# The first batch's local attention in blocks of 32 queries and 38 keys, its pooled part added in PSUM, and its q and k loaded as 1.5 KB rows

## The chip, the core and the metric

The kernel runs on one core of a Trainium2 chip. The metric is the device time of one execution in microseconds (us), as the median of the runs. The engines are named as in the profile: PE (TensorE: matmuls and transposes), PEld (its weight loads), DVE (VectorE), ACT (ScalarE), POOL (GpSimd), SP (SyncE, which here only issues DMAs). PSUM has eight banks; a matmul writes there, and DVE or ACT read it out.

## The reference

Eight batches of attention with 8 heads, 576 positions and 64 numbers a head, all float32; then a layer norm and a feed-forward network over the joined heads.

```python
B, H, S, D = q.shape                      # 8, 8, 576, 64; factor = 4
q_d = q.reshape(B, H, S // 4, 4, D).mean(axis=3)      # k_d and v_d likewise
out_up = np.repeat(sm_attn(q_d, k_d, v_d), 4, axis=2) # full attention on the pooled ones
mask = np.abs(pos[:, None] - pos[None, :]) < 4        # local attention: 7 neighbours
scores = np.where(mask, scale * (q @ k.T), -1e9)
out_local = softmax(scores) @ v
x = (out_up + out_local).transpose(0, 2, 1, 3).reshape(B, S, 512)
xn = (x - mu) / np.sqrt(var + 1e-6) * g_ln
out = x + np.maximum(xn @ w_ch1, 0.0) @ w_ch2         # 512 -> 2048 -> 512
```

The two weight matrices come as float64 and are turned into float32 pairs (a high and a low part) in the kernel.

## The kernel before

**The whole.** The 8 x 576 = 4608 rows of x are 36 tiles of 128 rows. The feed-forward network goes over them in chunks: chunk 0 has 4 tiles (rows 0 to 511, nearly all of batch 0), chunk 1 has 2, the others 3 each. In a chunk, `up` (products named h, L1279) and `down` (acc, L1303) go over 16 blocks of the 2048 hidden columns. In chunk 0 each block's weights are still to be loaded (tiles s) and converted (hi, lo on ACT, DVE and POOL). Attention of the later batches is done between the network's products.

**The order.** A class `Plan` collects tasks: an engine, an estimated duration, the tasks it needs, a due time, and rooms (buffers) taken and given back: "u" (2 KB buffers), "a" (the 8 PSUM banks), "e" (wide buffers), "xx". It lays them out by due times and costs and writes each engine's program in that fixed order; each engine then works through its list and waits on semaphores. Where its layout leaves a gap on PE, it puts warm-up matmuls of the identity there (L205). The DMAs on SP are issued in the order of the list too, and each also waits for the DMA eight before it.

**Batch 0.** It stands ahead of all else, since chunk 0 needs it. Its q and k are loaded by tokens (`own_tokens`, L472: 128 tokens by 8 heads, pieces of 64 numbers), turned on PE by transposes (L479), summed in fours on DVE for the pooled attention and copied to `reg` by ACT. Local attention (`window`) goes by windows of two blocks, 64 queries by 64 keys each: a mask product (L541), scores (L550), exponentials, transposes (L582), times v (`times_v`, L601, with a column of ones whose result is the sum), and a division on DVE or ACT. The pooled attention (scores gs L955, transposes gt L1006, times v gv L1021) gives od. Since the 64 keys of a block give 58 queries, the windows don't lie on tiles of x: `expand` picks the rows with a 0/1 matrix named choice (ex L1119) and adds the pooled rows, repeated by a 0/1 matrix named spread (L1128), in one PSUM bank. Rows 512 to 575, half of tile 4, go by DMA: pooled rows to DRAM (ud, L1049), and x<-xl (L1227).

**Batches 1 to 7** (`pair`: qr and kr loads L709, DVE transposes, ls L754, lt L803, lv L821, a store xs<-xl to DRAM) are not edited. DVE's L831 writes xl, which lies in a room "e".

Their and the network's lines move only by the file's length: L205 becomes L209, L709 L714, L1279 L1245, L1303 L1269.

Of the kernel before, what the change touches and what calls it, by code (L numbers as in the profile page):

```python
# [9 lines left out]
F32 = mybir.dt.float32  # L10
# [129 lines left out]
def attention_then_ffn(  # L140
# [42 lines left out]
    TOKENS = ((0, 128), (128, 128), (256, 96), (340, 128), (468, 108))  # L183
    CUT = TOKENS[3][0]
    GROUPS = (0, 32, 64, 85, 117, SD)
    NU -= sum(SEP.values())
    SHIFTED = (0, 1, 2, 3)
# [31 lines left out]
    mask_b = const.tile([P, 2, 64], mybir.dt.bfloat16, name="mask_b")  # L219
# [25 lines left out]
    def copy_masks():  # L245
        nc.vector.tensor_copy(mask_b, mask.unsqueeze(1).broadcast_to([P, 2, 64]))
        nc.vector.memset(mask_b[64:, 1, 63:], NEG)

    SEL, SEL0 = 128, 376
    box_sel = []  # L250

    def make_choice():
        t = unit([P, 512], "choice")
        box_sel.append(t)
        nc.gpsimd.memset(t, 0.0)
        for c0, c1, firsts in ((0, SEL0, (EDGE, EDGE)), (SEL0, SEL0 + P, (0, EDGE))):
            for par in range(2):
                m = t[64 * par : 64 * par + 64, c0:c1]
                at = (SEL if c0 == 0 else 0) + HOP * par
                nc.gpsimd.affine_select(  # L260
                    out=m, in_=m, compare_op=ALU.not_equal, fill=1.0, base=at, pattern=[[-1, c1 - c0]],
                    channel_multiplier=1,
                )
                for base, sgn in ((-firsts[par], 1), (HOP + EDGE - 1, -1)):
                    nc.gpsimd.affine_select(
                        out=m, in_=m, compare_op=ALU.is_ge, fill=0.0, base=base, pattern=[[0, c1 - c0]],
                        channel_multiplier=sgn,
                    )

    SPREAD_LAST = FACTOR * 2 * GB  # L270

    def make_spread():
        t = wide([P, SPREAD_LAST + 2 * P], "spread")
        box_sel.append(t)
        nc.gpsimd.memset(t, 0.0)
        half = SPREAD_LAST // 2
        for par, c0, n, first in (
            (0, 0, half, 0), (1, half, half, 0), (0, SPREAD_LAST, P, 64 - GB), (1, SPREAD_LAST + P, P, 64 - GB)
        ):
            m = t[64 * par : 64 * par + 64, c0 : c0 + n]  # L280
            nc.gpsimd.memset(m, 1.0)
            for sgn in (1, -1):
                nc.gpsimd.affine_select(
                    out=m, in_=m, compare_op=ALU.is_ge, fill=0.0, base=FACTOR * first if sgn > 0 else EDGE - FACTOR * first,
                    pattern=[[sgn, n]], channel_multiplier=-sgn * FACTOR,
                )
# [20 lines left out]
    def window_at(i):  # L307
        return norm_at(0) - B0W - B0W_GAP * (2 - i)

# [15 lines left out]
    B0W, B0W_GAP, B0G, B0G_GAP = 5, 3, 8, 1.5  # L325
# [5 lines left out]
    EARLY_DUE = 40  # L331
# [122 lines left out]
    xt, piece = {}, {}  # L454
    chosen, own_moves = {}, []
    reg, turned_own, sums_own, vp, vp_done = {}, {}, [], {}, []
    gs = {}

    def own_tokens(u, nm):
        src = q if nm == "q" else k  # L460
        t0, n = TOKENS[u]
        part = int(t0 >= CUT)
        off = t0 - (CUT if part else 0)
        g0, g1 = GROUPS[u], GROUPS[u + 1]
        due = window_at(max(u - 1, 0))
        add = plan.add
        x = SimpleNamespace()
        by_act = nm == "k" and u < BY_ACT

        def load():  # L470
            x.raw = unit([P, H, D], f"{nm}n{u}")
            (nc.scalar if by_act else nc.sync).dma_start(  # L472
                x.raw[:n], src[0, :, t0 : t0 + n, :].rearrange("h c d -> c h d")
            )

        def turn():
            x.p = psa(f"l{nm}{u}").rearrange("p (c t) -> p c t", c=NPAIR)
            for pr in range(NPAIR):
                nc.tensor.transpose(  # L479
                    x.p[:, pr, :n], x.raw[:n, 2 * pr : 2 * pr + 2].rearrange("p h d -> p (h d)"), ident[:n, :n]  # L480
                )

        def sums():
            if u == 0:
                gs[nm] = wide([P, NPAIR, SD], f"gs{nm}")
            nc.vector.tensor_reduce(
                out=gs[nm][:, :, g0:g1],
                in_=x.p[:, :, : FACTOR * (g1 - g0)].rearrange("p c (g r) -> p c g r", r=FACTOR),
                axis=AX.X, op=ALU.add,
            )  # L490

        def turn_out(copy):
            if off == 0:
                width = S + 1 - CUT if part else TOKENS[2][0] + TOKENS[2][1]
                reg[nm, part] = work.tile([P, NPAIR, width], F32, tag="xx", bufs=NX, name=f"r{nm}{part}")
                if part:
                    nc.gpsimd.memset(reg[nm, part][:, :, width - 1 :], 0.0)
            copy(reg[nm, part][:, :, off : off + n], x.p[:, :, :n])
# [9 lines left out]
    def own_v(pr):  # L508
# [3 lines left out]
        def ones_v():  # L512
            vp[pr] = wide([P, NBLK, D + 1], f"vp{pr}")
            nc.gpsimd.memset(vp[pr][:, :, D], 1.0)
# [888 lines left out]
```

## Time and profile before

| | |
|---|---|
| median of 3 runs | 972.67 us (970.27 to 974.83) |
| profiled execution | 971.22 us, its span 969.5 us |
| PE busy in the span | 949.3 us (98%) |
| DVE, ACT, POOL busy | 568.2 (59%), 285.5 (29%), 210.6 us (22%) |
| mean granted clock of PE | 0.995 |

The span runs from the first to the last instruction of the profiled execution; 1.7 us of its time lie around it. A busy share is a sum over stages: warm-up matmuls count as busy, and the first 150 us differ from the rest.

### The profile page before, as it was taken

Reading aid. Unit: us, or ns where it says so; the run is one execution under the profiler, and the core shown is the slowest. Engines: PE = TensorE matmul, PEld = TensorE weight load, DVE = VectorE, ACT = ScalarE, POOL = GpSimd, SP = SyncE. Lnnn points to the kernel's source line nnn. Section 1 sums busy time; section 2 is a strip of 40 time slices with the busy share of each in tenths; the row PEclk is TensorE's granted clock in tenths of the full one; section 3 lists DMA queues with packets and bytes.
Section 4 is the critical chain, followed back from the end, with each engine's and each line's share of the span. In section 5 each row is a group of like instructions: output and inputs, shape, how many; then the busy total and the mean of one; then the engine's idle time right before and its main releaser. Section 6 shows DMA issues by size and latency. Waiting matters only on the chain.

```text
span 969.5 us, 22589 instructions
## 1 busy us (share of the span) xinstructions
PE 949.3 (98%) x8742; PEld 852.9 (88%) x8742; DVE 568.2 (59%) x1363; ACT 285.5 (29%) x757; POOL 210.6 (22%) x395
## 2 busy tenths in 40 slices
PE   9898989999999999999999999999999999999998
PEld 8787878999889989889988989899989989999997
DVE  5499755767565757567477567768467443233212
ACT  4787854223123132113123112213113121212110
POOL 7325323333212212222111011232022001110000
PEclk9999989999999999999999999999999999999999
DMA  8998986687787849788677797997786565432400
GB/s 172 176 276 203 274 221 166 192 226 197 211 190 192 235 140 232 235 225 215 216 188 181 200 244 203 248 267 202 217 200 190 161 196 159 162 107 68 163 1 33
DMA packets 311299, 183.88 MB, mean 190 GB/s; under 512 B 197080, under 2 KB 264600, under 8 KB 311192
## 3 DMA queue, kind: packets, MB, share of 16 engines
q1 hardware_dynamic: 304648, 169.33, 65.8%
q0 software_dynamic: 3680, 12.39, 4.2%
q8 instruction: 69, 1.13, 0.5%
q10 hardware_dynamic: 2864, 0.72, 0.4%
q14 instruction: 38, 0.31, 0.1%
HBM read 139.91 MB, written 42.34 MB: 188 GB/s over the span
## 4 chain that ended last, share of the span: by engine, by line
PE 85%; DMA 1%; DVE 1%; SPq 0%; issue 0%; ACT 0%; DVEq 0%; ACTq 0%
PE h L1279 39%; PE acc L1303 39%; PE lv L821 2%; PE gv L1021 2%; PE ls L754 1%; PE gs L955 1%; PE gt L1006 1%; DMA xs<-xl 1%; DMA qr<-in_q_dram 0%; PE px L1183 0%; PE lt L803 0%; DVE x L1308 0%; PE h L205 0%; SPq L709 0%; DVE gmx L963 0%
## 5 line engine op out<-in xcount | busy, mean ns | idle before, releaser
L1303 PE MATMUL acc<-hi,hx 128*128 128x512 f32 x768 | 260.0, 392 | 0.0
L1290 DVE SCALAR_TENSOR_TENSOR hx<-h,hx 128x384 fp32r<-128x384 f32 (+1 forms) x176 | 95.6, 543 | 269.9 <-ACT hx L1287 269.5
L1287 ACT ACTIVATE hx<-h 128x384 fp32r<-128x384 f32 (+1 forms) x176 | 84.8, 482 | 556.1 <-PE h L1279 364.7
L1303 PEld LDWEIGHTS acc<-hi,hx 128*128 128x128 f32 x768 | 144.1, 188 | 28.8 <-issue 1.0
L1303 PE MATMUL acc<-lo,hx 128*128 128x512 f32 x384 | 151.2, 394 | 0.0
L1279 PE MATMUL h<-xh,lo 128*128 128x384 f32 (+1 forms) x656 | 135.8, 329 | 0.5 <-ACT xh L1188 0.5
L1279 PE MATMUL h<-xh,hi 128*128 128x384 f32 (+1 forms) x656 | 132.1, 323 | 0.0
L1279 PE MATMUL h<-xlo,hi 128*128 128x384 f32 (+1 forms) x656 | 131.6, 322 | 0.0
L1279 PEld LDWEIGHTS h<-xh,lo 128*128 128x128 f32 x656 | 111.4, 190 | 11.4 <-ACT xh L1188 0.7
L1279 PEld LDWEIGHTS h<-xh,hi 128*128 128x128 f32 x656 | 111.5, 189 | 0.0
L1279 PEld LDWEIGHTS h<-xlo,hi 128*128 128x128 f32 x656 | 109.7, 190 | 0.1
L1303 PE MATMUL acc<-w,hx 128*128 128x512 f32 x384 | 96.5, 395 | 0.0
L1303 PEld LDWEIGHTS acc<-w,hx 128*128 128x128 f32 x384 | 70.6, 188 | 13.7 <-issue 0.8
L1303 PEld LDWEIGHTS acc<-lo,hx 128*128 128x128 f32 x384 | 72.2, 188 | 9.7
L1138 POOL TENSOR_TENSOR x<-x,up 128x512 f32<-128x512 f32 x32 | 41.1, 1290 | 181.0 <-DMA x<-xs 119.0
L1279 PE MATMUL h<-xh,w 128*128 128x384 f32 (+1 forms) x352 | 67.7, 334 | 0.0
L1279 PEld LDWEIGHTS h<-xh,w 128*128 128x128 f32 x352 | 61.7, 188 | 3.3
L421 POOL TENSOR_TENSOR lo<-s,hi 128x512 fp32r<-128x512 f32 x27 | 36.4, 1355 | 65.9 <-ACT hi L416 47.1
L1188 ACT ACTIVATE xh<-xy,gain 128x128 fp32r<-128x128 f32 x108 | 34.8, 394 | 18.3 <-DVE xy L1175 17.5
L978 ACT ACTIVATE ag<-gs,gmx 128x192 f32<-128x192 f32 x96 | 32.0, 430 | 25.0 <-DVE lrp L829 9.6
L1152 POOL TENSOR_TENSOR mv<-mv,neg_half 128x1 f32<-128x1 f32 x36 | 21.8, 605 | 77.3 <-DVE mv L1149 61.1
L408 DVE SCALAR_TENSOR_TENSOR s<-s 128x256 int32<-128x256 int32 x64 | 35.3, 560 | 4.0 <-ACT s L400 2.0
(175 smaller groups left out, 1226.3 us busy)
## 6 DMA issues: line engine op xcount, KB each, us to landing
w<-w SPq DMA_DIRECT2D x148, 256.0 KB
s<-in_moe_w_ch_dram SPq DMA_DIRECT2D x64, 256.0 KB
out_dram<-x SPq DMA_DIRECT2D x36, 256.0 KB
vwp<-in_v_dram SPq DMA_DIRECT2D x54, 160.0 KB
qr<-in_q_dram SPq DMA_DIRECT2D x112, 72.0 KB
kr<-in_k_dram SPq DMA_DIRECT2D x112, 72.0 KB
up<-ud SPq DMA_DIRECT2D x28, 256.0 KB
x<-xs SPq DMA_DIRECT2D x28, 256.0 KB
```

The costliest lines, as they stand in the source:

```text
L408: nc.vector.scalar_tensor_tensor(out=x.raw[0][:, 256 * i : 256 * (i + 1)], in0=pairs[:, :, 1], scalar=3, in1=pairs[:, :, 0], op0=ALU.logic ...
L421: eng.tensor_sub(lo, x.raw[0].bitcast(F32), x.hi.bitcast(F32))
L821: nc.tensor.matmul(x.pv[h2][hs, w], lhsT=x.at[js, w, hs], rhs=x.v[js, 2 * w + par], start=True, stop=True)
L978: nc.scalar.activation(to, of, AF.Exp, scale=POOLED_SCALE, bias=y.mx[:, h2, c : c + 1])
L1021: nc.tensor.matmul(y.pv[h2][64 * n : 64 * n + 64, c], lhsT=y.at[kb][ks, c0 : c0 + 64], rhs=x.v[ks, kb, pr], start=kb == 0, stop=kb == 2,)
L1138: nc.gpsimd.tensor_add(xt[n], xt[n], x.up)
L1152: nc.gpsimd.tensor_tensor(x.mv[:, 1:2], x.mv[:, 1:2], neg_half, op=ALU.pow)
L1188: nc.scalar.activation(into(xh, kc), pxt[n][:, kc], AF.Copy, scale=gain[:, kc : kc + 1])
L1279: nc.tensor.matmul(out, lhsT=wt[:, kc], rhs=rhs, start=n == 0, stop=n == 3 * KC - 1)
L1287: nc.scalar.activation(hx[c, f][0], ph[c, f][:, :tokens], AF.Relu)
L1290: nc.vector.scalar_tensor_tensor(out=hx[c, f][1], in0=ph[c, f][:, :tokens], scalar=0.0, in1=hx[c, f][0].bitcast(F32), op0=ALU.max, op1=ALU ...
L1303: nc.tensor.matmul(acc[c][j], lhsT=lt[:, ts], rhs=rt, start=f == 0 and n == 0, stop=last and n == 2)
```

## The change

**Loads and turning.** `own_qk` loads q and k by head: 96 partitions hold 6 positions each, so a row is 6 x 64 numbers, 1.5 KB. There are 16 such DMAs (ten issued by SP, six by ACT). To get the 64 numbers on partitions, PE multiplies each of the six 64-column slices by the identity (L463), for two heads and in two pieces (partitions 0 to 63 and 64 to 95): 192 products, written to every sixth column of PSUM. DVE sums and ACT copies from there.

**Local attention.** `near_scores` takes 32 queries by 38 keys, four blocks to a window, so that a window is a tile of x: four windows of four blocks and one of two. It divides on DVE in SBUF before the transposes. `assembled` multiplies by v (L615) and adds the pooled rows by spread into the same PSUM bank (L622, L629); `keep` copies it to x. The choice matrix, `expand`, the DMAs to ud of batch 0 and x<-xl of tile 4 are gone. v comes in 16 pieces of 48 rows in two parts (18 DMAs, two of them on POOL). Two of the six poolings of v may go to DVE. Six planner constants change.

```diff
+    BQ, BK = 32, 32 + 2 * EDGE
+    PER = 6
+    RAW = S // PER
+    HIGH = 64
+    LEFT, CUT = 356, 348
+    SPLIT = (LEFT - BQ - EDGE) // BQ + 1
+    VROWS = 48
+    V_FIRST = 8
...
+    B0G, B0G_GAP = 20, 4
+    OWN_AT, OWN_V, OWN_V2, OWN_NEAR, OWN_GAP, OWN_END = -40.0, -2.0, 16.0, 10.0, 3.0, 4.0
...
-    EARLY_DUE = 40
+    EARLY_DUE = 25
...
-    LEAD1 = 40
+    LEAD1 = 35
...
-    G1 = 22
+    G1 = 20
...
-    W_GAP = 12
+    W_GAP = 13
...
+        def load(h2, by):
+            x.raw[h2] = unit([P, PER * D], f"{nm}n{pr}_{h2}")
+            by.dma_start(x.raw[h2][:RAW], src[0, 2 * pr + h2].rearrange("(g r) d -> g (r d)", r=PER))
+
+        def turn(n):
+            p0, p1 = ((0, HIGH), (HIGH, RAW))[n]
+            x.p[n] = psa(f"l{nm}{pr}_{n}")[:, : PER * (p1 - p0)]
+            for r in range(PER):
+                for h2 in range(2):
+                    nc.tensor.matmul(
+                        x.p[n][64 * h2 : 64 * h2 + 64].rearrange("p (g r) -> p g r", r=PER)[:, :, r],
+                        lhsT=x.raw[h2][p0:p1, r * D : (r + 1) * D], rhs=ident[p0:p1, p0:p1], start=True, stop=True,
+                    )
...
+            if n:
+                copy(reg[nm, 1][:, pr, PER * HIGH - CUT : S - CUT], x.p[n])
+            else:
+                copy(reg[nm, 0][:, pr, EDGE:], x.p[n][:, :LEFT])
+                copy(reg[nm, 1][:, pr, : PER * HIGH - CUT], x.p[n][:, CUT:])
...
+                q.dma_start(
+                    to[:VROWS, 1:], bass.AP(head.tensor, head.offset + (BQ - EDGE) * D, [[D, VROWS], [BQ * D, nb - 1], [1, D]])
+                )
+                return
+            q.dma_start(
+                to[:VROWS], bass.AP(head.tensor, head.offset + (BQ * m0 - EDGE) * D, [[D, VROWS], [BQ * D, nb], [1, D]])
+            )
...
-        def load():
-            x.raw = unit([P, H, D], f"{nm}n{u}")
-            (nc.scalar if by_act else nc.sync).dma_start(
-                x.raw[:n], src[0, :, t0 : t0 + n, :].rearrange("h c d -> c h d")
-            )
...
-        def turn():
-            x.p = psa(f"l{nm}{u}").rearrange("p (c t) -> p c t", c=NPAIR)
-            for pr in range(NPAIR):
-                nc.tensor.transpose(
-                    x.p[:, pr, :n], x.raw[:n, 2 * pr : 2 * pr + 2].rearrange("p h d -> p (h d)"), ident[:n, :n]
-                )
...
+                    x.ps[h2], lhsT=ident_b[:, :rows], rhs=near_b[:, variant].unsqueeze(1).broadcast_to([P, NPAIR, BK]),
                     start=True, stop=False,
                 )
...
-                    for par, c0 in enumerate(cols):
+                    for n, m in enumerate(blocks):
+                        part = int(m >= SPLIT)
+                        c0 = BQ * m - (CUT if part else -EDGE)
                         nc.tensor.matmul(
-                            x.ps[h2][64 * par : 64 * par + 64, pr], lhsT=qt[ds, pr, c0 : c0 + 64],
-                            rhs=kt[ds, pr, c0 : c0 + 64], start=False, stop=pr == NPAIR - 1,
+                            x.ps[h2][BQ * n : BQ * (n + 1), pr], lhsT=reg["q", part][ds, pr, c0 : c0 + BQ],
+                            rhs=reg["k", part][ds, pr, c0 - EDGE : c0 - EDGE + BK], start=False, stop=pr == NPAIR - 1,
                         )
...
+            nc.vector.reduce_sum(r, a, axis=AX.X)
+            nc.vector.tensor_scalar_add(r, r, 1e-9)
+            nc.vector.reciprocal(r, r)
+            nc.vector.tensor_mul(a, a, r.unsqueeze(2).broadcast_to([rows, H, BK]))
...
+                for h2 in range(2):
+                    js = slice(64 * h2, 64 * h2 + BK)
+                    for n, m in enumerate(blocks):
+                        part = int(m >= V_FIRST)
                         nc.tensor.matmul(
-                            x.pv[n][hs, pr], lhsT=x.at[js, pr, hs], rhs=vp[pr][js, blocks[m]], start=True, stop=True
+                            x.px[h2][BQ * n : BQ * (n + 1), pr], lhsT=x.at[js, pr, BQ * n : BQ * (n + 1)],
+                            rhs=vp[pr, part][js, m - V_FIRST * part], start=pr == 0, stop=False,
...
+            for h2 in range(2):
+                for hg in range(2):
+                    if i < 3:
+                        nc.tensor.matmul(
+                            x.px[h2][:, 2 * hg : 2 * hg + 2], lhsT=spread[0][:, i * P : i * P + rows],
+                            rhs=od[hg][:, :2, h2], start=False, stop=hg == 1,
+                        )
+                        continue
+                    for par in range(2):
+                        c0 = (S - 3 * P) * par + P * (i - 3)
+                        nc.tensor.matmul(
+                            x.px[h2][:, 2 * hg + par], lhsT=spread[1][:, c0 : c0 + rows], rhs=od[hg][:, 2, h2],
+                            start=False, stop=hg == 1 and par == 1,
+                        )
+
+        def keep():
+            xt[i] = unit([P, DM], f"x{i}")
+            for h2 in range(2):
+                nc.scalar.copy(xt[i][:rows].rearrange("p (c h d) -> p h c d", h=2, d=D)[:, h2], x.px[h2])
...
-                    nc.tensor.matmul(
-                        x.up[:, es], lhsT=box_sel[0][:, c0 : c0 + P], rhs=y.xl.rearrange("p h d -> p (h d)")[:, es],
-                        start=e == 0, stop=False,
-                    )
-                for pr in range(2 if n == NOWN - 1 else 1):
-                    c0, rhs, to = n * P, od[hg][:, :2], x.up[:, es]
-                    if n == NOWN - 1:
-                        c0, rhs = SPREAD_LAST + P * pr, od[hg][:, 2]
-                        to = x.up[:, hg * 256 + pr * P : hg * 256 + (pr + 1) * P]
-                    nc.tensor.matmul(to, lhsT=box_sel[1][:, c0 : c0 + P], rhs=rhs, start=False, stop=pr == 1 or n < NOWN - 1)
...
-                    def move(y=y, n1=n1, p0=p0, r0=r0, m=m):
-                        if n1 not in xt:
-                            xt[n1] = unit([P, DM], f"x{n1}")
-                        nc.sync.dma_start(xt[n1][p0 : p0 + m], y.xl[r0 : r0 + m].rearrange("p h d -> p (h d)"))
...
+        if n < NOWN:
+            t = kept_own[n]
```

**The start of PE's program.** k and q of the first group or pair are lk and lq; kn and qn are the loaded rows. Before:

```order
L205 MATMUL lk_140<-ident 128x128 x8
L479 MATMUL lk_140<-ident,kn_93 128x128 x4
L479 MATMUL lq_157<-ident,qn_95 128x128 x4
L205 MATMUL lk_170<-ident 128x128 x4
L479 MATMUL lk_170<-ident,kn_97 128x128 x4
L205 MATMUL lq_185<-ident 128x128 x4
L479 MATMUL lq_185<-ident,qn_99 128x128 x4
```

and after (twelve such products make a piece):

```order
L209 MATMUL lk_0_134<-ident 128x128 x8
L463 MATMUL lk_0_134<-ident,kn_0_83 64x64
L463 MATMUL lk_0_134<-ident,kn_1_81 64x64
L463 MATMUL lk_0_134<-ident,kn_0_83 64x64
L463 MATMUL lk_0_134<-ident,kn_1_81 64x64
```

The warm-up matmuls between the first turns are gone, and a piece of four transposes is now twelve products of 64 x 64 or 64 x 32.

**Where tile 0 of x is made, on PE.** at holds the turned attention, vp is v, od the pooled result; before, xl is the divided local result. Before:

```order
L582 MATMUL lt_812<-ident,la_618 128x128 x4
L582 MATMUL lt_817<-ident,la_712 128x128 x4
L1119 MATMUL ex_829<-xl_650,choice 128x256
L1119 MATMUL ex_829<-xl_710,choice 128x256
L1128 MATMUL ex_829<-od_769,spread 128x256
L1119 MATMUL ex_829<-xl_650,choice 128x256
```

and after:

```order
L615 MATMUL ex_0_916<-vp_0_85,at_871 32x64 x4
L615 MATMUL ex_1_917<-vp_0_85,at_871 32x64 x4
L615 MATMUL ex_0_916<-vp_0_523,at_871 32x64 x4
L615 MATMUL ex_1_917<-vp_0_523,at_871 32x64 x4
L615 MATMUL ex_0_916<-vp_0_565,at_871 32x64 x4
L615 MATMUL ex_1_917<-vp_0_565,at_871 32x64 x4
L615 MATMUL ex_0_916<-vp_0_575,at_871 32x64 x4
L615 MATMUL ex_1_917<-vp_0_575,at_871 32x64 x4
L622 MATMUL ex_0_916<-od_738,spread_169 128x128
L622 MATMUL ex_0_916<-od_858,spread_169 128x128
L622 MATMUL ex_1_917<-od_738,spread_169 128x128
L622 MATMUL ex_1_917<-od_858,spread_169 128x128
```

What was times v, a division elsewhere, and a selection is now 32 products of 32 x 64, with the four pooled products straight behind them.

**SP's queue behind the loads of v.** s_0 and s_1 are the first weight blocks, qr and kr are of batch 1. Before:

```order
L519 DMA vp_105<-in_v_dram 64x10x64 x2
L519 DMA vp_107<-in_v_dram 64x10x64 x2
L519 DMA vp_112<-in_v_dram 64x10x64 x2
L519 DMA vp_114<-in_v_dram 64x10x64 x2
L709 DMA qr_454<-in_q_dram 32x18x32 x4
L709 DMA kr_509<-in_k_dram 32x18x32 x4
L386 DMA s_0_0_556<-in_moe_w_ch_dram 128x2x256
L386 DMA s_0_1_557<-in_moe_w_ch_dram 128x2x256
```

and after:

```order
L534 DMA vp_1_585<-in_v_dram 48x10x64
L534 DMA vp_1_590<-in_v_dram 48x10x64
L534 DMA vp_1_631<-in_v_dram 48x10x64
L534 DMA vp_1_674<-in_v_dram 48x10x64
L376 DMA s_0_0_836<-in_moe_w_ch_dram 128x2x256
L376 DMA s_0_1_837<-in_moe_w_ch_dram 128x2x256
L376 DMA s_1_0_845<-in_moe_w_ch_dram 128x2x256
L376 DMA s_1_1_846<-in_moe_w_ch_dram 128x2x256
L714 DMA qr_866<-in_q_dram 32x18x32 x4
L714 DMA kr_961<-in_k_dram 32x18x32 x4
L381 DMA s_0_0_1057<-in_moe_w_ch_dram 128x512
L381 DMA s_0_1_1058<-in_moe_w_ch_dram 128x512
```

The first two blocks' weights now stand ahead of the loads of batch 1, and more DMAs stand ahead of both.

## Rows read from the trace of the kernel before

**Rows 1.** Busy times by stretch of the span: PE, PEld, DVE, ACT, POOL.
```profile
0.00:60.00 60.00, 54.03 (x874) 48.54 (x875) 36.88 (x109) 38.29 (x117) 28.99 (x91) 0.97 0.95 192
60.00:136.00 76.00, 69.86 (x759) 61.31 (x758) 63.40 (x143) 59.06 (x156) 32.49 (x34) 1.00 0.91 242
```

**Rows 2.** PE's waits, by what it waited for.
```profile
PE gt L1006 <- DVE lrp L829: 4.6, 2, 4.3
PE lv L601 <- DMA vp<-in_v_dram: 2.8, 3, 1.6
```

**Rows 3.** The warm-up matmuls (L205) by stretch; PE, PEld.
```profile
60.00:100.00 40.00, 3.37 (x24) 2.91 (x24) 1.00 0.93 237
...
sum 970.00, PE 23.32 PEld 21.29; mean PE 3.33 PEld 3.04
```

**Rows 4.** PE from the start to the network's first product: start, duration, instruction.
```profile
1.52 3.79 PE L205 MATMUL lk<-ident 128*128 128x128 f32 x16 [1.52 <-POOL ident masks.py:199]
5.09 1.06 PE L479 MATMUL lk<-ident,kn 128*128 128x128 f32 x4
...
7.14 1.06 PE L205 MATMUL lk<-ident 128*128 128x128 f32 x8
8.03 0.60 PE L479 MATMUL lk<-ident,kn 128*128 128x128 f32 x4
...
16.33 0.38 PE L541 MATMUL ls<-mask_b,ident_b 128*128 128x256 bf16 x2
16.65 0.70 PE L550 MATMUL ls<-rk,rq 64*64 64x64 f32 x32
17.27 0.59 PE L479 MATMUL lk<-ident,kn 108*128 108x108 f32 x4
...
19.90 1.70 PE L955 MATMUL gs<-gsk,gsq 64*64 64x144 f32 x48
...
24.86 1.15 PE L1006 MATMUL gt<-ident,ag 128*128 128x128 f32 x9
...
54.36 0.60 PE L1183 MATMUL px<-ident,xn 128*128 128x128 f32 x4
54.80 0.49 PE L803 MATMUL lt<-ident,la 128*128 128x128 f32 x3
...
59.40 0.74 PE L1279 MATMUL h<-xh,lo 128*128 128x256 f32 x4
```

**Rows 5.** gv of a later batch at full clock: min/median/max ns, first and last start.
```profile
L1021 PE MATMUL gv<-vd,agt x72: 217/218/268, 90.6 to 91.7; 64*64 64x65 f32 x72
```

**Rows 6.** Two stretches with the DMA rate: the last two columns are DMA share, GB/s.
```profile
10.00:20.00 10.00, 10.00 (x172) 9.03 (x174) 7.55 (x18) 5.24 (x12) 5.96 (x26) 1.00 0.97 198
...
50.00:60.00 10.00, 9.66 (x106) 8.89 (x105) 9.06 (x25) 8.76 (x30) 2.40 (x4) 1.00 1.06 270
```

**Rows 7.** SP's issues: start, time to issue.
```profile
21.93 5.54 SPq L519 DMA_DIRECT2D vp<-in_v_dram  x8
...
34.08 1.01 SPq L386 DMA_DIRECT2D s<-in_moe_w_ch_dram  x2
...
42.91 1.79 SPq L1049 DMA_DIRECT2D ud<-od  x4
...
60.78 2.22 SPq L1227 DMA_DIRECT2D x<-xl  x3
```

**Rows 8.** The chain of waits that ended last, at 135 us.
```profile
135.15 4.86 DMA xs<-xl
```

**Rows 9.** PE behind that: start, duration, instruction.
```profile
140.77 1.69 PE L1006 MATMUL gt<-ident,ag 128*128 128x128 f32 x6 [4.30 <-DVE lrp L829]
142.25 1.91 PE L205 MATMUL h<-ident 128*128 128x128 f32 x8
143.82 1.20 PE L1279 MATMUL h<-xh,lo 128*128 128x256 f32 x4
...
146.53 0.71 PE L1279 MATMUL h<-xh,lo 128*128 128x256 f32 x4
```

More of the change, by code (lines that the diff above doesn't have):

```diff
@@ L265, in make_choice @@
                     nc.gpsimd.affine_select(
-                        out=m, in_=m, compare_op=ALU.is_ge, fill=0.0, base=base, pattern=[[0, c1 - c0]],
-                        channel_multiplier=sgn,
-                    )
[L270 to L285, printed above, removed]
-                )
+                        out=m, in_=m, compare_op=ALU.is_ge, fill=0.0,
@@ L450, in again, with own_qk @@
                         alt=by_pool(2, load))
[L454 to L456 removed]
+    xt = {}
+    reg, turned_own, sums_own, vp, vp_done = {}, {}, {}, {}, {}
     gs = {}
[L459 removed]
+    def own_qk(pr, nm):
         src = q if nm == "q" else k
[L461 to L465, printed above, removed]
[L466 to L506 removed]
@@ new lines, in sums, with turn_out @@
+        def sums(n):
+            if nm not in gs:
+                gs[nm] = wide([P, NPAIR, SD], f"gs{nm}")
+            half = PER * HIGH // FACTOR
+            nc.vector.tensor_reduce(
+                out=gs[nm][:, pr, half:] if n else gs[nm][:, pr, :half],
+                in_=x.p[n].rearrange("p (g r) -> p g r", r=FACTOR), axis=AX.X, op=ALU.add,
+            )
+        def turn_out(n, copy):
+            if not pr and not n:
+                for part, width in ((0, EDGE + LEFT), (1, S + EDGE - CUT)):
+                    reg[nm, part] = work.tile([P, NPAIR, width], F32, tag="xx", bufs=NX, name=f"r{nm}{part}")
+                    pad = reg[nm, part][:, :, width - EDGE :] if part else reg[nm, part][:, :, :EDGE]
+                    nc.gpsimd.memset(pad, 0.0)
+            if n:
[3 more added lines that the diff above has]
+                copy(reg[nm, 1][:, pr, : PER * HIGH - CUT], x.p[n][:, CUT:])
@@ new lines, in near_scores, with zeros, scores @@
+    def near_scores(i):
+        add = plan.add
+        due = OWN_NEAR + OWN_GAP * i
+        x = SimpleNamespace()
+        blocks = [m for m in range(4 * i, 4 * i + 4) if m < S // BQ]
+        rows = BQ * len(blocks)
+        variant = 1 if i == 0 else 2 if i == NOWN else 0
+        def zeros():
+            x.a = unit([P, H, 64], f"la{i}")
+            nc.gpsimd.memset(x.a[:, :, BK:], 0.0)
+        def scores():
+            x.ps = [psa(f"ls{i}_{h2}")[:rows, : NPAIR * BK].rearrange("p (c j) -> p c j", c=NPAIR) for h2 in range(2)]
@@ new lines, in keep @@
+        def keep():
+            xt[i] = unit([P, DM], f"x{i}")
+            for h2 in range(2):
+                nc.scalar.copy(xt[i][:rows].rearrange("p (c h d) -> p h c d", h=2, d=D)[:, h2], x.px[h2])
+        t = add("POOL", 0.6, zeros, (), due - 3.0, take=U, ahead=AHEAD)
+        needs = [turned_own[nm, pr, n] for nm in "qk" for pr in range(NPAIR) for n in ((0,) if i < 2 else (0, 1))]
+        s = add("PE", 0.8, scores, needs + [near_done], due, take=(("a", 2),))
+        scored_own.append(s)
```

344 lines of the change are left out of this document (144 added, 200 removed).

## The prediction, made before the changed kernel had run

> **What bounds the kernel now.** I read the busy times by stretch first. PE is the bound: from 146 us to 940 us it is never idle, so there only its own work counts, and the change adds and removes nothing there. What can move is the time before 146 us. In the first 60 us PE is busy 54.03, that is idle 5.97, and from 60 to 136 us it is idle 6.14 of 76 [rows 1]. Second, the waits: the longest is gt behind DVE's division (4.3 us), and times v waits 2.8 us for v [rows 2]. Third, what is busy without being work: 23.32 us of warm-up matmuls, 3.37 of them between 60 and 100 us [rows 3]. Fourth, PE's instructions up to the first network product at 59.40 us [rows 4]. Fifth, the stall at 136 us: DVE's write of xl needs a room that a store to DRAM holds for 4.86 us [rows 8], PE stands 4.30 us, and what follows runs at about half speed: twelve h products take from 143.82 to 146.53 [rows 9]. So the reader should see some 40 us of waiting, warm-up and slow clock before 146 us, and only these and batch 0's own products are in play.
>
> **Term 1, to the first network product, worked out forward.** Almost everything of batch 0 is replaced, so I build the new prelude rather than take differences.
>
> *Loads of q and k.* 16 pieces of 147 KB are 2.36 MB. At 198 GB/s, the rate while the old short pieces loaded, that is 11.9 us, at 270, the rate of a later stretch, 8.7 [rows 6]. With a start at 2 us, about where PE's program begins, they have landed at 11 to 14 us.
>
> *Turning.* 192 float32 products; one such product is two instructions on PE (the first eight warm-ups show as 16 [rows 4]), so 384. The trace has no 64 x 64 or 64 x 32 product written to every sixth column. The nearest are the scores of 64 x 64: 32 of them from 16.65 to 17.27, 19.4 ns each [rows 4]; from below the 64 x 65 products of gv, 72 in some 1.1 us (90.6 to 91.7), about 16 ns [rows 5]; from above gs with 64 x 144, 1.70 us for 48, 35 ns [rows 4]. They are nearest to the first, so 7.4 us, bounds 6 to 13.6. Behind the cold warm-up, which ends at 5.09, that is 12.5; with the loads I take **13.0** for the last turn.
>
> *Local and pooled attention.* Four windows of 64 instructions and one of 32, both for scores (32 x 38) and times v (32 x 64): 288 each, at 19.4 ns 5.6 us each. Mask products for five windows, 0.32 each by the start of the next row (16.33 to 16.65; now 152 columns instead of 256, so an upper bound): 1.6. gs 1.70 and gt 2 x 1.15 as they are; gv 144 at the clock of [rows 5], 2.6. Transposes: five of attention and three of px, 0.44 each (54.36 to 54.80): 3.5. The pooled part in PSUM: 24 instructions of 128 columns at 0.111 (the eight warm-ups from 7.14 to 8.03), 2.7, and 32 of 64 columns, between the 16 ns and the 0.111, at half of the latter 1.8. All of this is 27.4 us [rows 4, 5]. Of 29 warm-up products behind the first eight in the whole new order, 25 lie here: 50 instructions at 0.111, 5.6 us. So 13.0 + 27.4 + 5.6 = 46.0 with no wait.
>
> *Waits.* Before, PE waited 4.0 us between 10 and 60 us (5.97 less the 1.52 and 0.45 at the start), 2.8 of it for v. v's first part is now issued behind more DMAs of q and k but shorter ones: the old queue was through with v at 27.47 (21.93 + 5.54) [rows 7]; I estimate 24 to 26.5, and the first product that needs v comes at about 29. So that wait goes. What is late next is the chain on DVE: a window's maximum, subtraction and four operations of the division, now all before the transposes. DVE was busy 36.88 of 60 us [rows 1], so it has room, but PE's order is fixed and each of five windows can make it wait. I take 2 us, bounds 0 to 6. First network product at **48.0** instead of 59.40: **11.4 us earlier**.
>
> **Term 2, from there to 136 us.** Batch 1's first pair (40 scores and 40 times v at 19.4 ns, five transposes) stood before the first network product and now stands behind it: 2.1 us back. In place of 32 warm-up instructions behind the first network product (24 in [rows 3], eight in [rows 9]) there are eight: 24 x 0.111 = 2.7 gained. The six us of idle in this stretch are waits for batch 1's chain. I leave them unchanged; bounds are minus 4 and plus 6, because the loads don't come 11 us earlier. On SP the store to ud (1.79) and x<-xl (2.22) fall away [rows 7], and v is through 1 to 3.5 us earlier: 5 to 7.5 us in all. What covers the rest: the first weight block was issued at 34.08 and used at 59.40 [rows 4, 7]; now it is issued ahead of batch 1's q and k, at about 25, and used at 48, so the 25 us between become 23. Without that cover the cost is the difference of 11.4 and 5 to 7.5. DVE is the engine to watch here, with 63.40 of 76 us busy [rows 1].
>
> **Term 3, the stall.** At stake: 4.30 idle, and at half speed 0.7 (six gt in 1.48, where nine take 1.15 at most [rows 4]), 0.7 (warm-up, 1.57 against 0.89) and 1.35 (half of 2.71): 7.0 us [rows 4, 9]. In the new order DVE's write of that xl waits for no DMA any more, since batch 0 gives its wide rooms back earlier; but other room waits are new (the stores and loads on SP now wait for PE and ACT in more places). I take half, **3.5**, bounds 0 and 7.
>
> **What costs nothing.** ACT's copies out of PSUM come in more and shorter pieces and two poolings of v can lie on DVE; both engines stand idle much of the first 40 us, covered by the waits for loads. If that cover is gone it is term 1's wait. The two DMAs moved to POOL's queue stand there behind its first additions and are needed only by the third window.
>
> **Sum.** 11.4 - 2.1 + 2.7 + 3.5 = 15.5. The profiled execution took 971.22 us (1.7 outside its span), so 955.7; it lay 1.45 below the median of the runs, so for a median I say **957**.
>
> [...] The small products are the point: there are 960 of them on PE (384 + 288 + 288), and the trace has 19.4 ns for one [rows 4]. [...]
>
> **Rivals.**
> *A, more comes.* The idle between 60 and 136 us falls by 4 and the stall goes wholly (3.5 more): 15.5 + 7.5 = 23, so 949 to 950. For it: those waits are for batch 1 and DVE, and DVE has an earlier start. Against: its loads are only 5 to 7.5 us earlier. Chance 0.2.
> *B, the loads set the pace.* Chunk 0 can't run further ahead than SP's list: 5 to 7.5 us are kept, and the stall stays in another place: gain about 6.5, **966**. For it: the DMA share of 0.91 and DVE's busy share in that stretch [rows 1]. Against: the 25 us between issue and use. Chance 0.2.
> *C, slower: the small products cost by the instruction.* If one costs 35 ns, as gs does [rows 4], the 960 take 15 us more, and the gain is gone (972). From 34 to 36 ns on it decides; at 55 ns, half the 0.111 of a 128-column one, it is 34 us more, less 15.5, so 991. For it: a third tile size and strided writes, neither in the trace. Against: 64 x 65 at 16 and 64 x 64 at 19.4, so width is not what is paid there. [...] Chance 0.09, two thirds of it beyond the bound.
> *D, nothing comes.* A new chain (mask, scores, maximum, subtraction, exponential, division, turn, times v) in a fixed order makes PE wait as long as before: 2 + 11 us of waits in term 1, 968 to 973. Chance 0.08.
>
> **Numbers.** The forecast has 0.43 (952 to 962). 0.5% of the median is 4.9 us, about what a measurement of this kernel can tell from no change: faster is below 967.8. Faster: the forecast, A and B, 0.83, and a little of D, 0.85. Same: most of D and a third of C, 0.09; slower 0.06. The range from 946 to 968 leaves out C, D and the far end of A, 2 in 10.
>
> **What would show it.** The last L463 at about 13 us, the first L1245 at 46 to 52; L463, L571 and L615 at 16 to 22 ns from start to start; no wait for vp; no idle over 2 us near 120 to 130 us; warm-ups at 11 to 12 us of busy time; PE never idle behind chunk 0 except for the tail. It is wrong if those products stand at 30 ns or more, if ls of batch 1 waits for lkt by several us (B), or if a stall like that of [rows 9] comes back under another name.

## The result and the profile after

The changed kernel took **984.06 us** (980.57 to 986.56, 4 runs) where the kernel before took 971.47 beside it: ratio 1.0122, interval 1.0078 to 1.0167. It is slower by 1.2%, outside the range. The profiled execution took 980.57 us, its span is 978.8. It is the fastest of the four; the 3.5 us by which the median is longer stand in no trace. Busy times, and the clock in 40 slices of the span (the kernel before has 0.97 to 60 us [rows 1]):

```profile
PE 955.6 (98%) x9268; PEld 859.4 (88%) x9268; DVE 569.5 (58%) x1377; ACT 278.0 (28%) x738; POOL 212.4 (22%) x403
...
PEclk7789999999999999999999999999999999999999
```

The view by stretches (columns as in [rows 1], then clock, DMA share, GB/s):

```profile
0.00:60.00 60.00, 52.43 (x1167) 47.84 (x1167) 26.82 (x86) 21.62 (x67) 19.52 (x74) 0.72 0.92 186
60.00:136.00 76.00, 68.13 (x845) 60.54 (x847) 64.49 (x152) 57.85 (x161) 33.24 (x43) 0.98 0.81 215
136.00:184.00 48.00, 48.00 (x500) 43.02 (x497) 34.57 (x79) 27.89 (x71) 15.30 (x14) 1.00 0.75 193
```

The reader sees 1167 instructions on PE in the first 60 us, where there were 874, at a mean clock of 0.72 where it was 0.97. DVE and ACT have less to do in this stretch than before. From 136 to 184 us, where the stall of [rows 9] was, PE has no idle time. PE's timeline to the first network product, which answers to [rows 4] (start, duration, instruction, idle time before it):

```profile
5.22 1.43 PE L463 MATMUL lk<-ident,kn 64*64 64x64 f32 x24
...
16.74 2.96 PE L463 MATMUL lk<-ident,kn 64*64 64x64 f32 x48
...
23.69 1.47 PE L463 MATMUL lq<-ident,qn 32*64 32x32 f32 x24
25.09 3.16 PE L961 MATMUL gs<-gsk,gsq 64*64 64x144 f32 x48
...
32.90 0.77 PE L571 MATMUL ls<-rk,rq 64*32 64x38 f32 x64
...
41.34 0.47 PE L571 MATMUL ls<-rk,rq 64*32 64x38 f32 x22 [3.34 <-issue]
...
51.14 1.06 PE L615 MATMUL ex<-vp,at 38*32 38x64 f32 x51 [1.89 <-issue]
...
68.27 0.43 PE L600 MATMUL lt<-ident,la 64*128 64x64 f32 x4 [2.25 <-ACT s L390]
...
71.79 0.72 PE L1245 MATMUL h<-xh,lo 128*128 128x256 f32 x4
```

The first network product starts at 71.79 instead of 59.40, 12.4 us later. The turns end at 25.09; in most of them 48 instructions take 2.9 us, 60 ns each. The scores are quick (64 in 0.70, 11 ns), but twice a group of small products breaks off and PE stands with nothing to wait for ("issue"). PE's waits behind 185 us, where the kernel before has none:

```profile
PE lv L826 <- issue: 1.8, 1, 1.8
PE lv L826 <- DVE at L797: 1.1, 1, 1.1
PE h L1245 <- DVE hx L1256: 0.6, 1, 0.6
```

**Where the 9.3 us of span went.** +12.4 to the first network product. From there to px of tiles 4 and 5, the end of chunk 0 (183.52; 179.06 before), -7.9: the stall of [rows 9] is gone. From there to the end 795.3 instead of 790.4, +4.8, for the same instructions. 12.4 - 7.9 + 4.8 = 9.3.

### The profile page after: what moved, and what is told of

Its sections match the earlier page's. It is cut to its first block, busy times and chain, and to the rows that moved or that the text cites. A ratio compares the mean times of both kernels' runs of the same rounds, so it can differ in the third digit from the quotient of the medians.

```text
span 978.8 us, 23700 instructions
## 1 busy us (share of the span) xinstructions
PE 955.6 (98%) x9268; PEld 859.4 (88%) x9268; DVE 569.5 (58%) x1377; ACT 278.0 (28%) x738; POOL 212.4 (22%) x403
## 4 chain that ended last, share of the span: by engine, by line
PE 86%; DMA 2%; DVE 1%; ACT 0%; issue 0%; POOL 0%; SPq 0%; DVEq 0%; ACTq 0%; POOLq 0%
PE acc L1269 39%; PE h L1245 39%; PE lv L826 2%; PE gv L1027 2%; PE ls L759 2%; PE gs L961 1%; DMA x<-xs 1%; DMA ad<-la 1%; PE lt L808 1%; PE gt L1012 1%; DMA ar<-ad 0%; POOL x L1123 0%; PE px L1164 0%; DVE st L1127 0%; ACT la L783 0%
## 5 line engine op out<-in xcount | busy, mean ns | idle before, releaser
L1123 POOL TENSOR_TENSOR x<-x,up 128x512 f32<-128x512 f32 (+1 forms) x32 | 41.3, 1292 | 200.8 <-DMA x<-xs 152.2
L411 POOL TENSOR_TENSOR lo<-s,hi 128x512 fp32r<-128x512 f32 x26 | 34.6, 1335 | 62.0 <-ACT hi L406 42.3
L984 ACT ACTIVATE ag<-gs,gmx 128x192 f32<-128x192 f32 x96 | 32.0, 428 | 28.3 <-DVE lrp L834 16.4
L1245 PE MATMUL h<-xlo,w 128*128 128x384 f32 (+1 forms) x176 | 36.8, 330 | 0.0
```

Source lines behind the costliest of these rows:

```text
L411: eng.tensor_sub(lo, x.raw[0].bitcast(F32), x.hi.bitcast(F32))
L984: nc.scalar.activation(to, of, AF.Exp, scale=POOLED_SCALE, bias=y.mx[:, h2, c : c + 1])
L1123: nc.gpsimd.tensor_add(xt[n][p0:], xt[n][p0:], x.up[p0:])
L1245: nc.tensor.matmul(out, lhsT=wt[:, kc], rhs=rhs, start=n == 0, stop=n == 3 * KC - 1)
```

## The experiments

**1. q and k by tokens again**, the rest of the change kept (128 x 128 transposes, loads in short pieces as before).

```diff
-            by.dma_start(x.raw[h2][:RAW], src[0, 2 * pr + h2].rearrange("(g r) d -> g (r d)", r=PER))
+                x.raw[:n], src[0, :, t0 : t0 + n, :].rearrange("h c d -> c h d")
...
+                nc.tensor.transpose(
+                    x.p[:, pr, :n], x.raw[:n, 2 * pr : 2 * pr + 2].rearrange("p h d -> p (h d)"), ident[:n, :n]
+                )
```

> Changed kernel, but q and k loaded by tokens and turned by transposes of 128 x 128 as before the change; the new local attention, the pooled part in PSUM and the constants stay (the layout is made anew, with its own warm-ups). Theory, clock: in the changed kernel PE falls to half clock at 10 us among the turning products, and most of the 12 us by which the first network product comes later (71.8 against 59.4) is these products and the half clock behind them. Then here PE stays at full clock to about 30 us, the last turn ends at 16 to 18 instead of 25.1 us, the first network product comes at 60 to 64, and the time is 970 to 976. Rival, the chain: the new local attention with its fixed order of DVE, ACT and PE and the two waits that the trace calls issue set the time; then the first network product stays at 69 to 72 and the time at 981 to 985.

Measured 976.81 us, ratio 1.0033 (1.0019 to 1.0047). The last turn comes at 17.9, the first network product at 67.88. So the turning can't be all of the loss: this kernel has 344 turning instructions less (40 for 384), and the first network product comes only 3.9 us earlier, not at the 60 to 64 of the theory, since stops of issue appear in place of the turns:

```profile
PE gv L1018 <- issue: 4.3, 1, 4.3
PE ex L606 <- issue: 2.9, 1, 2.9
PE gs L952 <- issue: 2.2, 1, 2.2
```

The profiled spans differ by 3.2 us, the ratios by some 8.7: more than half of the gain is seen in no trace, so how much of it the turning made stays open.

**2. Only the rows**: the kernel before with the new loads and turns, its own local attention.

> Kernel before, with only the loads of q and k in 1.5 KB rows and their turning by products taken from the change; windows of 64 queries, choice matrix and constants stay as before. Theory: the turning (two parts of the array) costs 384 x 34 ns and more at half clock, and every window has to wait for all four head pairs; last turn at 20 to 26 us, first network product at 64 to 69 instead of 59.4, time 976 to 983. With the new local attention alone at 3.7 us over before, both together would make the 12 us. Rival: the loads in long rows land earlier and give it back, time within 2 us of before.

978.42 us, ratio 1.0066 (1.0031 to 1.0102). Alone, the rows cost some 0.7% and the rest of the change (experiment 1: local attention, loads of v, constants) 0.3%, 1.0% together, which fits the change's 1.2% within the intervals: both parts lose. (Only the timed ratio is used here.)

**3. Warm-ups among the turns**, two products ahead of each of the 16 pieces, to hold the clock.

```diff
+            for _ in range(2):
+                nc.tensor.matmul(x.p[n][:, :P], lhsT=ident, rhs=ident, start=True, stop=True)
```

> Changed kernel with two warm-up matmuls of 128 x 128 (four instructions, 0.45 us at full clock) ahead of each of the 16 turning pieces: 7.1 us more work on PE. Theory, clock: PE stays at full clock through the turning, a turning instruction takes 30 to 34 ns instead of 60, the last turn ends at 24 to 26 us in spite of the added work, and gs behind it takes 1.7 instead of 3.2 us; time 978 to 984, not slower than the changed kernel. Rival, instruction count alone: a turning instruction takes as long as before and the 7 us come on top, time 988 to 992.

984.14 us, ratio 1.0128 (1.009 to 1.0167): no change. Its timeline:

```profile
26.31 0.89 PE L465 MATMUL lk<-ident,kn 32*64 32x32 f32 x24
27.13 0.71 PE L462 MATMUL lq<-ident 128*128 128x128 f32 x4
27.77 0.89 PE L465 MATMUL lq<-ident,qn 32*64 32x32 f32 x24
28.58 1.70 PE L963 MATMUL gs<-gsk,gsq 64*64 64x144 f32 x48
```

At full clock (1.00 granted from 20 to 30 us) 24 turns take 0.82 from start to start, 34 ns each, and gs is back at 1.70. The clock is worth what the warm-ups cost (16 x 0.65 = 10 us), and the first network product is at 71.04. Even at full clock the price is that of rival C. Whether transposes of the same slices, one instruction on PE as in [rows 4] instead of the two of a product, would halve the turning was not measured.

**4. The kernel before without its warm-ups** (`WARM` 150 to 4).

> Kernel before without its warm-up matmuls, but for the first eight. Theory, clock: the warm-ups kept PE's clock up in the first 60 us; without them it falls to half among the turns and the local attention, and the time is longer by 3 to 10 us although 19 us of PE's busy time are gone. Rival: they lay in waits and kept nothing, so time and clock stay as they are (within 2 us).

971.95 us beside 973.14, ratio **0.9985** (0.9973 to 0.9998). Its clock falls to 0.83 in the first 20 us, and yet its first network product comes at 57.51, 1.9 earlier. The warm-ups of the kernel before bought nothing, and this is the one version that beats it, barely.

**5. The products by themselves.** No loads; the output is zeros. Streams of 384 instructions on two parts of the array (64 x 64, into every sixth column or into neighbouring ones) and on four parts, then 1536 of 64 x 38 on eight parts, each behind 96 warm-up instructions.

> None of the reference's work: streams of small float32 products alone, with no other DMA beside them and 96 instructions of 128 x 128 ahead of each stream: 192 products in the turning's form (two parts of the array, every sixth column), 192 of the same to neighbouring columns, 192 on four parts of the array, 768 products in the scores' form (32 x 38 on eight parts). The output is zeros. Theory: 34 ns an instruction on two parts, strided or not; 17 to 20 on four; 10 to 12 on eight, and the long stream of these stops for some microsecond about every 128 to 256 instructions, while the slower streams don't. Rival, strided writes: neighbouring columns take well under 34 ns. Rival to the supply of instructions: no stops in the long stream without other DMAs.

```profile
14.51 11.41 PE L216 MATMUL two_strided<-ident,raw 64*64 64x64 f32 x384
...
36.77 11.41 PE L224 MATMUL two_flat<-ident,raw 64*64 64x64 f32 x384
...
59.03 3.02 PE L232 MATMUL four<-ident,raw 64*64 64x64 f32 x191
63.21 2.09 PE L232 MATMUL four<-ident,raw 64*64 64x64 f32 x128 [1.15 <-issue]
...
78.67 2.12 PE L241 MATMUL eight<-raw 64*32 64x38 f32 x223
83.31 1.31 PE L241 MATMUL eight<-raw 64*32 64x38 f32 x128 [2.52 <-issue]
87.04 1.61 PE L241 MATMUL eight<-raw 64*32 64x38 f32 x128 [2.42 <-issue]
90.50 1.61 PE L241 MATMUL eight<-raw 64*32 64x38 f32 x128 [1.84 <-issue]
```

Two things stand here. The price goes by how many parts of the array take turns: 29.7 ns on two and 16 on four for the same 64 x 64, 9.5 on eight (these are smaller too); the stride costs nothing. And on four and eight parts such a pace lasts for some 200 instructions only (191 and 223): then come exactly 128, a stop of 1.2 to 2.5 us, 128, and so on. On eight parts 128 take 3.45 to 4.0 us, 3.6 on average or 28 ns each, in a kernel without any other load, and also where the granted clock has fallen to 0.50 (from 87 us on). The DMA view of 78 to 95 us has only this:

```profile
q8 instruction: 4, 0.07, 1.4%
```

Four packets of 0.07 MB together, so some 17 KB for 128 instructions on PE and their 128 weight loads. They fall at about 80.6, 84.0, 87.8 and 91.2 us, each some 3 us ahead of a block (at 83.31, 87.04, 90.50 and 93.95): PE stands for its program. In the whole kernel that queue has 23 packets, 0.38 MB, for 3072 instructions on PE and 3072 weight loads, one packet for 267. The changed kernel has 73 packets there, 1.20 MB, so 16.4 KB each, for 9268 and 9268, one for 254.

**6. Half of the small products**: scores and times v of every second head are left out (288 of 576 instructions), so half of local attention isn't computed.

```diff
-                for h2 in range(2):
+                for h2 in range(1):
                     ds = slice(64 * h2, 64 * h2 + 64)
```

> Changed kernel without half of the products of local attention: the scores (32 x 38) and the times v (32 x 64) of every second head are left out, 288 instructions of 576, so the output is not the reference's. Everything else, waits and layout, stays. Theory, instruction supply: the waits of PE that the trace calls issue, 3.3, 1.9 and 0.4 us before the first network product, come while PE runs dry of instructions, since 16 KB of them are fetched by DMA and these short products use them up in less than a fetch takes; then they fall together from 5.6 to under 3 us, and with 3.5 us of products gone the first network product comes 4 to 8 us earlier, time 976 to 981. Rival: these waits are something else, they stay at 5 us and more, the first network product comes at most 4 us earlier.

975.99 us, ratio 1.0023 (1.0007 to 1.004). First network product at 65.45, 6.3 earlier: 22 ns for each instruction left out, twice the 11 ns that one takes in a burst. The stops of issue ahead of it fall from 5.6 to 2.5 us. So half of what a small product costs here is its duration (288 at 11 ns are 3.2 us), half the stops (3.1). One thing in this trace doesn't fit: 48 turns take 2.96 us and gs 3.16, as at half clock in the change, but the granted clock stands at 1.00 to 27 us. No run settles which of the two is right there.

**7. Turns on four parts, both pieces of a pair interleaved** (64-row and 32-row products alternate).

> Changed kernel, but the two pieces of a head pair (rows 0 to 63 and rows 64 to 95 of the array) are turned together, their products in turn, so that consecutive products lie on four parts of the array instead of two. Nothing else moves but what the layout makes of it. What the runs showed so far: a turning instruction takes 34 ns at full clock whether 64 or 32 columns wide, on two parts of the array; scores of 64 x 64 on four parts took 19.4, scores of 32 x 38 on eight parts 11. Theory, parts of the array: an instruction waits for the one before it on the same part, some 70 ns at full clock, so four parts halve it: 17 to 20 ns, the turning takes 7 to 8 us at full clock, the last turn at 13 to 17 us instead of 25.1. If the turning's length is what came later, the first network product comes 6 to 11 us earlier than 71.8 and the time is 974 to 979. Rival, a price by the instruction or by the strided write: 30 us and more per thousand as before, no change in the last turn, time 982 to 986.

1032.55 us, ratio 1.0611 (1.0581 to 1.0641): a large miss. Each pair took

```profile
30.21 9.03 PE L465 MATMUL lq<-ident,qn 64*64 64x64 f32 x48
```

188 ns an instruction, at a granted clock of 0.50 (34 ns was the price at 1.00). The next two kernels ask why.

**8. The sizes by themselves**: the order of the change (24 instructions on 64 rows, 24 on 32) and the alternating one, nothing else running.

> None of the reference's work, zeros as output: the 192 turning products alone with the changed kernel's sizes, first in its order (twelve with 64 rows, twelve with 32), then back and forth between 64 and 32 rows on four parts. Theory, sizes: 30 to 35 ns an instruction in the first stream, over 100 in the second although no other engine or DMA works. Rival: both take 30 or less, and what cost 188 ns in the kernel was the SBUF or PSUM traffic beside it.

```profile
14.35 19.50 PE L217 MATMUL apart<-ident,raw 64*64 64x64 f32 x384
...
47.59 70.35 PE L217 MATMUL mixed<-ident,raw 64*64 64x64 f32 x384
```

51 ns an instruction apart, 183 mixed, but these means mix clocks: mixed, 22 instructions take 2.4 us at a granted clock of 1.00, 109 ns each, and 311 take 58 us at 0.50, 186 ns each; apart it is 36 to 37 and 56 to 60 (below). So at either clock going from 64-row to 32-row products and back costs three times as much (109 against 36 to 37, 186 against 56 to 60). What PE does at a change of size isn't seen in the trace. The first stream is nearly the change's own order, and it loses the clock by itself:

```profile
14.00:17.00 3.00, 3.00 (x81) 2.71 (x81) 0.00 (x0) 0.00 (x0) 1.00 0.00 0
17.00:20.00 3.00, 3.00 (x84) 2.85 (x84) 0.00 (x0) 0.00 (x0) 0.90 0.02 5
20.00:25.00 5.00, 5.00 (x89) 4.70 (x86) 0.00 (x0) 0.00 (x0) 0.50 0.00 0
```

That is 36 to 37 ns while the clock is 1.00 to 0.90, then 56 to 60 at 0.50, while 11.4 us of 64-row products alone (experiment 5) stayed at 1.00.

**9. Four parts of one size**: the second piece takes 64 rows too, of which DVE clears 32.

```diff
+            nc.vector.memset(x.raw[h2][RAW:], 0.0)
...
+                            lhsT=x.raw[h2][p0 : p0 + 64, r * D : (r + 1) * D], rhs=ident[p0 : p0 + 64, p0:p1], start=True, stop=True,
```

> As the run on four parts of the array, which made a turning instruction 188 ns, but with all products of one size in rows: the second piece is taken with rows 64 to 127 (rows 96 to 127 set to zero by DVE beforehand) instead of 64 to 95. Theory, sizes: what cost 188 ns was going back and forth between parts of 64 and of 32 rows; products of one size on four parts took 16 ns alone, in stops for instructions 27 ns on average. Then the turning takes 7 to 11 us, the last turn stands at 13 to 17 us, the first network product 6 to 10 us earlier than the changed kernel's 71.8, time 974 to 979. Rival: reading the raw tiles or writing two banks in turn is what cost 188; then the time is 1020 and more.

979.32 us, ratio 1.0084 (1.0053 to 1.0116). Where the clock is full, 48 instructions take 0.7 to 0.9 us, 15 to 18 ns, near the 19.4 that the prediction had taken for them, and the turns end at 17.2 instead of 25.1. But the stops of issue grow to 8.9 us, and the first network product is at 64.44.

**10. The same without warm-ups, and experiment 1 without warm-ups** (`WARM` 4), since each warm-up instruction has to be brought in too (one packet for 254 to 267 instructions, experiment 5).

> The same without warm-up matmuls but for the first eight. Theory, supply of instructions: the warm-ups take instructions and PE time and buy little, as in the kernel before (0.15% without them); time 1 to 3 us below the run with them, 972 to 977. Rival, clock: with more of small products the clock stays at half to 60 us and the time is 2 us and more above the run with them.

> The run with q and k loaded by tokens, without warm-ups but for the first eight. In that run PE waited 9.4 us for instructions before the first network product (2.2, 4.3 and 2.9). Theory, supply: 130 fewer products ahead of it make these waits shorter by 2 us or more, time 972 to 976. Rival, clock: half clock from 10 us on, and 977 to 981.

977.34 us, ratio 1.007 (1.0047 to 1.0093), and 975.48, ratio 1.004 (1.0021 to 1.0059). The first network products are at 61.30 and 62.67 (3.1 and 5.2 earlier), but the times hardly move. Against the change, 10.5 and 9.1 us ahead of the first network product come through as about 5 and 8. Nor do the stops of issue shrink each time that instructions go: without warm-ups they are 9.5 us instead of 8.9 with four parts, 3.4 instead of 9.4 by tokens. A warm-up instruction takes 111 ns [rows 4] and its supply some 28 (experiment 5), so by this estimate a warm-up can give the supply time rather than take it.

**11. The old planner constants**, in four layouts.

```diff
-    EARLY_DUE = 25
+    EARLY_DUE = 40
...
-    LEAD1 = 35
+    LEAD1 = 40
...
-    G1 = 20
+    G1 = 22
...
-    W_GAP = 13
+    W_GAP = 12
```

> The changed kernel with the four planner constants that the change altered set back to the values of before; products, loads and their order in the first batch stay. Theory (layout): the 4.8 us lost behind the first batch (waits of 3.5 us on VectorE, ScalarE and issue behind 185 us, where before has none) come from the plan that the new constants lay out, so they go with the old ones: 978 to 981 us, and waits of under 1 us behind 185 us. Rival: any new layout of the first batch brings such waits, as the kernel with only the rows changed has 4.4 us of them under the old constants: 982 to 986 us, and over 2 us of waits there.

> The four-parts turning of one size without warm-ups, with the four planner constants of before as well. Theory (layout): the waits behind 185 us go, so the gain in front of the first network product that this version has over the change stays and nothing is given back: 970 to 974 us. Rival: the waits stay, or others come in their place: 975 to 979 us.

> The kernel with q and k by tokens and without warm-ups (ratio 1.0040 before), with the four planner constants of before as well. Theory (constants): as with the four parts, the old constants bring about 6 us: ratio 0.996 to 0.999, 969 to 971 us. Rival (chance of a layout): what a constant is worth depends on the layout it meets, as the changed kernel gained nothing by the same four: ratio 1.002 to 1.008, 974 to 980 us.

> The changed kernel, turning on two parts as it does, with the four planner constants of before and without warm-ups. Theory (instructions): without the warm-ups' 100 and more instructions the supply has less to bring ahead of the first network product, and the constants help as they did with the four parts: 977 to 980 us, first network product at 67 to 69 us. Rival: the warm-ups were neutral as they were in the kernel before, so the time stays at 983 to 986 us and the first product at 71 to 73 us.

| layout | new constants | old constants |
|---|---|---|
| the change | 1.0122 (1.0078 to 1.0167) | 1.0139 (1.0083 to 1.0195) |
| the change, no warm-ups | not run | 1.0106 (1.0086 to 1.0126) |
| four parts, no warm-ups | 1.0070 (1.0047 to 1.0093) | **1.0009** (0.9993 to 1.0025) |
| tokens, no warm-ups | 1.0040 (1.0021 to 1.0059) | 1.0035 (1.002 to 1.005) |

The theory that the constants by themselves cost the 4.8 us fell in the first row: with the old ones the lost time came back as another wait, in the network's products at 210 us, for DVE's write of an xl as before the stall of [rows 9]:

```profile
209.95 0.72 PE L1245 MATMUL h<-xh,lo 128*128 128x256 f32 x4 [3.92 <-DVE xl L836]
```

With four parts they brought 6 us and the time of the kernel before, though its waits behind 185 us stay (2.8 us; its profiled execution, 975.30, was the slowest of its ten). Its first network product comes at 68.78, 7.5 us later than with the new constants, and the profiled spans are only 1.1 us apart, so where the six lie isn't seen. With tokens they brought nothing. The change without warm-ups missed both of its expectations: its first network product comes at 74.97, with 10.0 us of stops of issue ahead of it where the same kernel with warm-ups has 1.9, and its interval overlaps that kernel's. So for the constants the rival held: what they are worth depends on the layout. In the version that reaches the time of before, the turns look like this:

```profile
8.32 0.89 PE L466 MATMUL lq<-ident,qn 64*64 64x32 f32 x48
9.29 0.91 PE L466 MATMUL lk<-ident,kn 64*64 64x64 f32 x14
12.20 0.71 PE L466 MATMUL lk<-ident,kn 64*64 64x32 f32 x34 [1.99 <-issue]
12.70 0.91 PE L466 MATMUL lq<-ident,qn 64*64 64x32 f32 x48
13.40 0.88 PE L466 MATMUL lk<-ident,kn 64*64 64x32 f32 x44
16.43 0.30 PE L466 MATMUL lk<-ident,kn 64*64 64x64 f32 x4 [2.15 <-issue]
```

Between the two stops lie 34 + 48 + 44 = 126 instructions, and the trace can miss some: again the 128 of experiment 5.

## Why the prediction was wrong, step by step

**Term 1 failed: 12.4 us later, not 11.4 earlier, a miss of 23.8.** Four pieces make it up.

- *Turning: 25.1 instead of 13.0, 12.1 of it.* This is the step that failed: 19.4 ns for an instruction, taken from scores that go over four parts of the array [rows 4]. The turns of one head pair and piece use two parts, and there an instruction costs 29.7 ns alone, 36 to 37 with both sizes, 24 of each in a row, and 34 in the kernel at full clock (experiments 5, 8, 3). At 34 the 384 would take 13.1 us instead of 7.4, some 5 of the 12.1. The other 7 are the clock, which I took as full: it fell at about 10 us, and to 25 us an instruction took 60 ns. The row that I set aside, gs at 35 ns, was nearer only by chance: gs goes over four parts, with 144 columns. The loads weren't the limit: SP had issued its last q and k at 8.2.
- *Stops of issue: 5.6 us that no term had* (3.34, 1.89 and one of 0.35). I priced each group by its duration, as if PE's program were always there. Half of the products took 3.1 us of these stops with them (experiment 6). From the start to the first network product PE has 1335 instructions instead of 869. On average that is one in 54 ns, slower than the 28 of the supply, so the supply binds in the bursts and not over the whole stretch.
- *Waits: 3.1 us against the 2 that I took* (2.25 behind ACT's conversion of weights, 0.84 for the pooled ag).
- *The same work, much of it at half clock, about 5 us.* From 25.1 to 71.8 are 46.7 us, 8.7 of it idle; 38.0 against 27.4 + 5.6. gs alone took 3.16 instead of 1.70. This is what is left over, clock and wrong prices together; no run splits it. The scores, 11 ns, were cheaper than I said.

**v.** The wait for vp is gone, as I said, but not for my reason: SP is through with v at 31.4, not at 24 to 26.5, and PE now needs it only at 46.9. So the first weight block went out at 31.45, where I had about 25. SP's rows:

```profile
7.45 0.78 SPq L456 DMA_DIRECT2D qn<-in_q_dram  x2
...
20.23 11.18 SPq L534 DMA_DIRECT2D vp<-in_v_dram  x13
31.45 3.08 SPq L376 DMA_DIRECT2D s<-in_moe_w_ch_dram  x4
34.58 4.34 SPq L714 DMA_DIRECT2D qr<-in_q_dram  x4
```

**Terms 2 and 3 were right in sign and too small.** 7.9 us came back between the first network product and the end of chunk 0, where I had -2.1 + 2.7 + 3.5 = 4.1. The stall at 136 us is gone altogether. One long wait is left there, lt behind ACT (3.81 at 98.71). Warm-ups take 12.8 us, near my 11 to 12. Part of this gain may only be the delay itself, since a product that comes later waits less; no run tells the two apart. No ls of batch 1 waits for lkt, the sign of rival B.

**Behind chunk 0** I had said that the change adds nothing. It adds 4.8 us, 3.5 of them in the three waits shown. The rows of the two old-constant layouts show that other plans have such waits in other places. Which step of the plan makes them isn't settled: the profiles are of one execution each, no single constant was varied, and the wait of 1.8 for issue has no transfer of program ahead of it in the trace.

**Rival C was the answer, in part.** "Cost by the instruction" and its 34 to 36 ns were met in the turns, and missed in the scores, which cost 11. The chance of 0.09 rested on 64 x 65 at 16 ns and 64 x 64 at 19.4, and both are bursts on four parts. By themselves too, starts in a burst come 16 ns apart on four parts and 9.5 on eight, against 29.7 on two (experiment 5). That a long run of small products comes to 28 ns here is the supply, another cause. What is really paid here is parts of the array, clock, and supply of program.

## What to carry to other kernels

Price a small product not by its size but by three things read from rows that share them: how many parts of the array the group goes round, which clock its stretch has, and how many short instructions PE needs in a row, with 28 ns for each beyond some 200 (experiment 5). Don't trade a few large transposes for many small products (here 40 instructions for 384) ahead of everything else, and don't alternate 64-row and 32-row products (109 ns each against 36 to 37, experiment 8). A gain ahead of chunk 0 is only worth what the rest of the fixed order lets through: the version that reaches the time of before has its first network product 9.4 us later. Measure the whole.

## What the hardware showed that was not expected

- PE's program comes in blocks of 128 instructions with their weight loads; a block takes about 3.6 us when PE has run ahead (stops of 1.8 to 2.5 us), even with no other DMA (experiment 5).
- Alternating 64-row and 32-row products costs 109 ns each at full clock, against 36 to 37 with 24 at a time, and 186 against 56 to 60 at half.
- The clock fell from 1.00 to 0.50 while PE was busy without a gap, in the change's order of small products (experiment 8), and not in 11.4 us of 64-row ones (experiment 5). In experiment 8 it fell between 17 and 20 us in a stream begun at 14.35, sooner than the 64-row stream was long, so the length alone isn't it; whether the 32-row pieces or the changes of size do it wasn't tried.
- Warm-ups that held the clock at 0.97 in the kernel before were worth nothing: without them it is 0.15% faster (0.02 to 0.27).
